# An opening phase in another order: transposes on PE, new load order, x kept in load order

## The chip, the cores and the metric

The kernel runs on one core of one Trainium2 chip. The metric is device time in microseconds (us) of one execution. A core has five engines that run side by side, each strictly in its own order: PE (TensorE, matrix products), DVE (VectorE), ACT (ScalarE), POOL (GpSimd) and SP (SyncE). Here SP issues the plain loads, the stores and the DMA transposes, and POOL issues the loads that change fp32 to bf16 on the way. Work on different engines meets only where one waits for another.

## What is computed

Attention with normalized q and k, and then a feed-forward network with a product in place of an activation. There are 8 batches, 12 heads, 448 tokens and 64 numbers per head; the network has 768 inputs, an inner size of 1,024 and 3,584 tokens.

```python
def rmsnorm(x, g):
    rms = np.sqrt(np.mean(x * x, axis=-1, keepdims=True) + 1e-06)
    return x / rms * g
q_n, k_n = (rmsnorm(q, g_q), rmsnorm(k, g_k))
scores = scale * np.matmul(q_n, k_n.transpose(0, 1, 3, 2))
attn = softmax(scores)                      # written out in the reference
x = np.matmul(attn, v)                      # heads side by side: [3584, 768]
a = x @ w1
b = x @ w2
h = a * b @ w3
return (h @ w_out).astype(np.float32)
```

## The kernel before

**Quads.** Four heads of one batch are a quad; there are 24, three per batch. q and k of a quad are loaded in fp32 as [112, 4 heads, 4, 64] (L86): partition p holds the tokens 4p to 4p+3, so that a token is 4p + j. All score and probability tiles have their columns in the order j, p.

**Preparation of a quad**, in two halves of two heads: squares on POOL (L133; for quad 0 on ACT, L131), their sums on DVE (L136), the inverse root as a logarithm and an exponential on ACT (L141, L143), and the scaling on DVE in three operations (L152, L159, L165), which leaves `qks` in bf16 with tokens on partitions. A DMA transpose from SP (L171) turns it into `qkT`.

**Attention.** A quad has four slots. In each, `qk_exp` makes eight score products (two tiles `sc`, L185) and two exponentials on ACT into P (L194). In the first three slots `pv_set` of the quad before runs (L209): set 0 gives the sums of P, sets 1 and 2 give P times v, which DVE multiplies by the inverse sums into `xT` (L225). This write also changes the columns from the order j, p to the order of the tokens, 4p + j.

**The weights.** w3 and w_out are multiplied first, in 16 units of eight products (`w34_unit`, L240), cast by DVE to `w34s` (L247). For that w3 has to be transposed; eight DMA transposes do it (L353).

**The feed-forward work** is a list of fillers: once the third quad of a batch is through, 16 units of x with w1 or w2 (L254, L271) and the units of the last product (L293) come onto the list, and each slot takes two. DVE copies the result to `o_sb` (L300) and SP stores 128 rows (L303).

**Order.** It is written by hand, and each engine runs its part of it in this order. Before the loop stand quads 0 and 1 and the w3 transposes. Inside the loop quad i's slots hold the preparation of quad i + 2, the loads of q and k of quad i + 3 and of v of quad i + 2. The w34 units run two per slot in quads 1 and 2, fillers from quad 4 on:

```python
        W34_FROM = 1
        FFN_FROM = 4
```

Loads of w1 and w2 (L103) stand on POOL between the squares, four per slot. q, k and v tiles have three and four buffers, the squares two, and the PSUM tiles of w34 units and fillers share two (`mm`). Every eighth load of a queue uses the same semaphore, and an issue waits for the load eight places ahead of it.

## Time and profile before

| | |
|---|---|
| median of 2 runs | 455.52 us (454.74 to 456.31) |
| profiled execution | 451.86 us, its span 450.1 us |
| PE busy | 375.2 us, 83% of the span |
| DVE busy | 288.9 us, 64% |
| ACT busy | 232.5 us, 52% |
| POOL busy | 132.3 us, 29% |
| granted TensorE clock, mean | 0.977 |

The span goes from the first to the last instruction. A busy share is an average over stages that have different limits, so the stages are read apart. In a row of instructions the first number is the start in us from the span's start, then the duration, the engine, the line of the kernel, the operation with what it writes and reads, and how many instructions were merged; in brackets stands how long the engine was idle just before, and what ended that. Issues on SP and POOL show how long the issuing engine was held, not the transfer. Row durations of merged matmuls overlap a little, since matmuls are pipelined.

### The profile page before, as it was taken

What the parts mean: (1) busy time and instruction counts of PE and PEld (TensorE: products, weight loads), DVE (VectorE), ACT (ScalarE), POOL (GpSimd) and SP (SyncE); (2) the same over time, 40 slices, a digit from 0 to 9 for tenths busy, and PEclk for the clock granted to TensorE, in tenths of its full rate; (3) what the DMA queues carried; (4) which work ended last, traced back from release to release, by engine and by line L of the source; (5) the groups of instructions that cost most, each with busy time, mean ns of one, the idle gap of its engine ahead of it and who ended that gap; (6) DMA issues with size and microseconds to landing.
All of it is one profiled execution on the core that took longest, in us unless ns stands there. A gap on an engine that the chain in (4) does not pass through costs nothing.

```text
span 450.1 us, 7194 instructions
## 1 busy us (share of the span) xinstructions
PE 375.2 (83%) x2880; PEld 171.1 (38%) x2880; DVE 288.9 (64%) x380; ACT 232.5 (52%) x357; POOL 132.3 (29%) x148
## 2 busy tenths in 40 slices
PE   0002190796999999999999999999999999999996
PEld 0000040343344544444444444444444454445453
DVE  0531500879577888788877888788888787534333
ACT  3002330456766577556755675568566755673110
POOL 5260802522444124412442144214432340000000
PEclk9999996799799999999999999999999999999999
DMA  8999999555936755686458546954695462201003
GB/s 164 229 176 187 197 175 210 104 119 102 181 36 128 192 115 107 125 231 141 84 118 232 118 75 148 233 121 72 145 215 126 88 167 92 42 0 71 36 0 140
DMA packets 94753, 58.98 MB, mean 131 GB/s; under 512 B 55296, under 2 KB 88576, under 8 KB 94720
## 3 DMA queue, kind: packets, MB, share of 16 engines
q1 hardware_dynamic: 79552, 46.21, 44.3%
q0 software_dynamic: 15168, 12.32, 18.8%
q8 instruction: 22, 0.36, 0.3%
q14 instruction: 11, 0.09, 0.1%
HBM read 46.72 MB, written 11.01 MB: 128 GB/s over the span
## 4 chain that ended last, share of the span: by engine, by line
PE 67%; DMA 10%; DVE 9%; ACT 6%; SPq 4%; POOL 2%; issue 1%; DVEq 0%; POOLq 0%
PE po L293 17%; PE pa L254 14%; PE pb L271 14%; PE pv L209 10%; PE sc L185 8%; ACT P L194 5%; DMA k_sb<-in_k_dram 4%; DVE ssq L136 4%; PE wps L240 4%; DMA w2s<-in_moe_w_dram 2%; DVE xT L225 2%; DMA gk_b<-in_g_k_dram 2%; SPq L353 2%; SPq L171 1%; DVE abT L278 1%; POOL sq L133 1%
## 5 line engine op out<-in xcount | busy, mean ns | idle before, releaser
L194 ACT ACTIVATE P<-sc 112x896 bf16<-112x896 f32 x192 | 164.7, 914 | 59.0 <-PE sc L185 59.0
L185 PE MATMUL sc<-qkT 64*112 64x448 bf16 x384 | 63.1, 387 | 55.4 <-DMA qkT<-qks 33.2
L254 PE MATMUL pa<-xT,w1s 128*128 128x448 bf16 x384 | 85.4, 357 | 2.3 <-DVE xT L225 2.1
L271 PE MATMUL pb<-xT,w2s 128*128 128x448 bf16 x384 | 83.1, 352 | 0.0
L278 DVE TENSOR_TENSOR abT<-pb,a_sb 128x448 bf16<-128x448 f32 x64 | 39.9, 623 | 67.2 <-PE pb L271 46.1
L136 DVE TENSOR_REDUCE ssq<-sq 112x16 f32<-112x1024 f32 x48 | 58.0, 1209 | 34.6 <-POOL sq L133 34.6
L293 PE MATMUL po<-w34s,abT 128*128 128x384 bf16 x448 | 77.1, 326 | 0.1
L97 POOL DMA_DIRECT2D v_sb<-in_v_dram x24 | 18.0, 751 | 183.8 <-PE pv L209 149.2
L141 ACT ACTIVATE lnv<-ssq,eps_t 112x32 f32<-112x32 f32 x24 | 7.7, 321 | 107.8 <-DVE ssq L136 107.8
L133 POOL TENSOR_TENSOR sq<-q_sb 112x512 f32<-112x512 f32 x46 | 49.8, 1083 | 29.6 <-DMA q_sb<-in_q_dram 29.4
L225 DVE TENSOR_TENSOR xT<-pv,r 128x448 bf16<-128x448 f32 x48 | 55.2, 1154 | 3.2 <-PE pv L209 3.2
L185 PEld LDWEIGHTS <-qkT 64*112 64x112 bf16 x384 | 20.2, 127 | 94.8 <-issue 61.6
L293 PEld LDWEIGHTS <-abT 128*128 128x128 bf16 x448 | 42.1, 98 | 34.2 <-issue 8.3
L133 POOL TENSOR_TENSOR sq<-k_sb 112x512 f32<-112x512 f32 x46 | 50.7, 1102 | 7.1 <-DMA k_sb<-in_k_dram 6.9
L152 DVE TENSOR_TENSOR qtmp<-q_sb,alpha 112x512 bf16<-112x512 f32 x48 | 51.1, 1064 | 1.9 <-ACT alpha L143 1.9
L271 PEld LDWEIGHTS <-w2s 128*128 128x128 bf16 x384 | 37.6, 98 | 38.2 <-issue 3.8
L254 PEld LDWEIGHTS <-w1s 128*128 128x128 bf16 x384 | 33.6, 98 | 45.4 <-issue 21.0
L262 ACT CAST a_sb<-pa 128x448 bf16<-128x448 f32 x64 | 34.1, 532 | 26.9 <-PE pa L254 26.9
L209 PE MATMUL pv<-P,v_sb 112*32 112x448 bf16 x768 | 44.9, 355 | 0.0
L300 DVE COPY o_sb<-po 128x384 f32<-128x384 f32 x56 | 30.7, 555 | 21.6 <-PE po L293 21.3
L240 PE MATMUL wps<-w_outs,w3T 128*128 128x384 bf16 x128 | 25.6, 360 | 13.2 <-DVE w34s L247 13.2
L165 DVE TENSOR_TENSOR qks<-k_sb,alpha 112x512 bf16<-112x512 f32 x48 | 36.2, 755 | 0.0
(24 smaller groups left out, 149.9 us busy)
## 6 DMA issues: line engine op xcount, KB each, us to landing
q_sb<-in_q_dram SPq DMA_DIRECT2D x24, 448.0 KB, 4.8
k_sb<-in_k_dram SPq DMA_DIRECT2D x24, 448.0 KB, 5.6
out_dram<-o_sb SPq DMA_DIRECT2D x28, 384.0 KB, 2.7
v_sb<-in_v_dram POOLq DMA_DIRECT2D x24, 224.0 KB, 3.9
w3s<-in_moe_w_dram POOLq DMA_DIRECT2D x8, 256.0 KB, 15.4
w_outs<-in_moe_w_out_dram POOLq DMA_DIRECT2D x4, 384.0 KB, 13.9
w1s<-in_moe_w_dram POOLq DMA_DIRECT2D x8, 192.0 KB, 11.3
w2s<-in_moe_w_dram POOLq DMA_DIRECT2D x8, 192.0 KB, 10.8
```

Source lines behind the costliest of these rows:

```text
L133: nc.gpsimd.tensor_tensor(out=sq[:, t], in0=src[:, hs], in1=src[:, hs], op=MULT)
L136: nc.vector.tensor_reduce(out=s["ssq"][:, :, hs, :], in_=sq, axis=AX, op=ADD)
L152: nc.vector.tensor_tensor(out=qtmp.transpose([0, 2, 1, 3]), in0=s["q"][:, hs], in1=alpha[:, 0, hs].unsqueeze(3).broadcast_to([NP, 2, J, D] ...
L185: nc.tensor.matmul(out=sc[:, u, 0:S], lhsT=qkT[u * D : (u + 1) * D, pr, J + jk, :], rhs=qkT[u * D : (u + 1) * D, pr, 0:J, :].rearrange("d ...
L194: nc.scalar.activation(out=P[:, 2 * pr : 2 * pr + 2, jk, :], in_=sc[:, :, 0:S], func=AF.Exp)
L209: nc.tensor.matmul(out=ps[h * HALF : (h + 1) * HALF, :], lhsT=w, rhs=P[:, h, jk, :], start=(jk == 0), stop=(jk == J - 1), tile_position=(0 ...
L225: nc.vector.tensor_tensor(out=xT[b][:, 2 * m + kind - 1, :].rearrange("d (p j) -> d j p", j=J), in0=ps.rearrange("d (j p) -> d j p", j=J), ...
L240: nc.tensor.matmul(out=ps[:, 0:NH], lhsT=w3T[:, gc, fc * 128 : (fc + 1) * 128], rhs=w_outs[:, gc, nh * NH : (nh + 1) * NH], start=(gc == 0 ...
L254: nc.tensor.matmul(out=ps[:, 0:S], lhsT=w1s[:, c, fi * 128 : (fi + 1) * 128], rhs=xT[b][:, c, :], start=(c == 0), stop=(c == CM - 1),)
L271: nc.tensor.matmul(out=ps[:, 0:S], lhsT=w2s[:, c, fi * 128 : (fi + 1) * 128], rhs=xT[b][:, c, :], start=(c == 0), stop=(c == CM - 1),)
L278: nc.vector.tensor_tensor(out=abT[bp][:, fi, odd * S : (odd + 1) * S], in0=ps[:, 0:S], in1=a_tiles.pop((b, fi)), op=MULT,)
L293: nc.tensor.matmul(out=ps[:, 0:NH], lhsT=abT[bp][:, fi, t * 128 : (t + 1) * 128], rhs=w34s[:, fi, nh * NH : (nh + 1) * NH], start=(fi == 0 ...
```

## The change

- The gains `g_q` and `g_k` are loaded first; quad 0's loads come in halves of two heads; q and k of quads 1 and 2 follow before the loop.
- For quads 0 to 3 the DMA transpose is replaced by 8 PE transposes per half into a PSUM tile and one DVE copy (`prep_pe_transpose`); later quads keep the DMA transpose. The identity for that is made on POOL behind the w_outs loads.
- The eight DMA transposes of w3 are replaced by 8 x 8 PE transposes and eight DVE copies (`w3_transpose`), each one slot ahead of the units that use it.
- Quad 1 is prepared in quad 0's slots, quad 2 in quad 1's, quads 3 and 4 in quad 2's; from then on i + 2 as before. v of quad i + 1 is loaded in quad i.
- The w34 units run from quad 1's third slot to quad 3's second, one w3 transpose and two units per slot. Fillers run from quad 3's third slot on.
- Four loads of w3, and w1 and w2 in turn, stand on POOL two per slot.
- `xT` is written in the order j, p, without permuting. The output rows are then put in place by the stores: each tile of 128 columns is cut where j changes, and each of the two pieces writes rows that lie four rows apart.

```diff
+    out_r = out.rearrange("(b p j) n -> b j p n", b=B, j=J)
-        nc.sync.dma_start_transpose(
-            out=s["qkT"][:, pr], in_=qks.rearrange("p t j h d -> p (t j h d)")
-        )
+        if pe:
+            s["qks", pr] = qks
+        else:
+            nc.sync.dma_start_transpose(
+                out=s["qkT"][:, pr], in_=qks.rearrange("p t j h d -> p (t j h d)")
+            )
+
+    def prep_pe_transpose(i, pr):
+        s = st[i]
+        qks = s.pop(("qks", pr))
+        ps = mm_psum.tile([128, 2 * J, NP], BF, tag="mm", name="qkT_ps")
+        for t in range(2):
+            for j in range(J):
+                nc.tensor.transpose(
+                    ps[:, t * J + j, :], qks[:, t, j], ident[0:NP, 0:NP]
+                )
+        nc.vector.tensor_copy(out=s["qkT"][:, pr], in_=ps)
...
-            out=xT[b][:, 2 * m + kind - 1, :].rearrange("d (p j) -> d j p", j=J),
-            in0=ps.rearrange("d (j p) -> d j p", j=J),
-            in1=s["r"].rearrange("d (j p) -> d j p", j=J),
-            op=MULT,
+            out=xT[b][:, 2 * m + kind - 1, :], in0=ps, in1=s["r"], op=MULT
...
+    def w3_transpose(fc):
+        ps = mm_psum.tile([128, CF, 128], BF, tag="mm", name="w3T_ps")
+        for gc in range(CF):
+            nc.tensor.transpose(
+                ps[:, gc, :], w3s[:, fc, gc * 128 : (gc + 1) * 128], ident
+            )
+        nc.vector.tensor_copy(out=w3T[:, :, fc * 128 : (fc + 1) * 128], in_=ps)
...
-            r0 = bp * TOK2 + t * 128
-            nc.sync.dma_start(out=out[r0 : r0 + 128, :], in_=o_sb)
+            c0 = t * 128
+            while c0 < (t + 1) * 128:
+                c1 = min((c0 // NP + 1) * NP, (t + 1) * 128)
+                bb, j = divmod(c0 // NP, J)
+                p0 = c0 % NP
+                nc.sync.dma_start(
+                    out=out_r[2 * bp + bb, j, p0 : p0 + c1 - c0, :],
+                    in_=o_sb[c0 - t * 128 : c1 - t * 128, :],
+                )
+                c0 = c1
...
+        wq = [lambda c=c: load_w3(c) for c in range(4, CF)]
+        W34_FROM = (1, 2)
...
+            preps = []
+            if i < 3:
+                preps.append(i + 1)
+            if 2 <= i and i + 2 < NQ:
+                preps.append(i + 2)
...
+                if (i, sl) >= W34_FROM and fc_next[0] < CF:
+                    fc = fc_next[0]
+                    if fc == 0:
+                        w3_transpose(0)
+                    if fc + 1 < CF:
+                        w3_transpose(fc + 1)
+                    w34_unit(fc, 0)
+                    w34_unit(fc, 1)
+                    fc_next[0] += 1
+                else:
+                    fill(2)
```

Two places show the order that results. First POOL, from the loads ahead of the loop to the squares of quad 1 (`sq`; `v_sb`, `w3s` are the load targets). The brackets name what an issue waits for: DMASW with a number is the semaphore of an earlier load from POOL, DMAHW of one from SP. Before:

```order
L111 DMA w3s<-in_moe_w_dram 128x1024 x3
L111 DMA w3s<-in_moe_w_dram 128x1024 [waits DMASW0_49]
L111 DMA w3s<-in_moe_w_dram 128x1024 [waits DMASW1_49]
L111 DMA w3s<-in_moe_w_dram 128x1024 [waits DMASW2_49]
L111 DMA w3s<-in_moe_w_dram 128x1024 [waits DMASW3_49]
L111 DMA w3s<-in_moe_w_dram 128x1024 [waits DMASW4_49]
L133 ISA
L133 TENSOR_TENSOR sq<-q_sb 112x512 [waits DMAHW4_49,DVE_49]
L133 TENSOR_TENSOR sq<-k_sb 112x512 [waits DMAHW5_49]
```

After:

```order
L117 DMA w3s<-in_moe_w_dram 128x1024 x3
L117 DMA w3s<-in_moe_w_dram 128x1024 [waits DMASW0_49]
L103 DMA v_sb<-in_v_dram 112x4x256 [waits DMASW1_49]
L139 TENSOR_TENSOR sq<-q_sb 112x512 [waits DMAHW6_49,DVE_49]
L139 TENSOR_TENSOR sq<-k_sb 112x512 [waits DMAHW7_49]
L117 DMA w3s<-in_moe_w_dram 128x1024 [waits DMASW2_49]
L117 DMA w3s<-in_moe_w_dram 128x1024 [waits DMASW3_49]
L139 TENSOR_TENSOR sq<-q_sb 112x512 [waits DVE_49]
L139 TENSOR_TENSOR sq<-k_sb 112x512
L117 DMA w3s<-in_moe_w_dram 128x1024 [waits DMASW4_49]
L117 DMA w3s<-in_moe_w_dram 128x1024 [waits DMASW5_49]
```

Quad 1's squares stood behind all eight w3s loads and together; now they stand in two pairs between the w3s loads, the second pair behind the sixth.

Second DVE, where the weight products begin. Before, in the slots of quad 1 (`w34s` is the cast of a product, `ssq` the sums of squares, `qtmp` and `qks` the scaling):

```order
L247 CAST w34s<-wps 128x384 x2
L136 TENSOR_REDUCE ssq<-sq 112x2x8
L225 TENSOR_TENSOR xT<-pv,r 128x4x112
L247 CAST w34s<-wps 128x384 x2
L136 TENSOR_REDUCE ssq<-sq 112x2x8
L225 TENSOR_TENSOR xT<-pv,r 128x4x112
L247 CAST w34s<-wps 128x384 x2
L152 TENSOR_TENSOR qtmp<-q_sb,alpha 112x2x4x64
L159 TENSOR_TENSOR qks<-qtmp,g_b 112x512
L165 TENSOR_TENSOR qks<-k_sb,alpha 112x2x4x64
```

After, in the last three slots of quad 1 (`qkT_ps` and `w3T_ps` are the PSUM tiles of the PE transposes):

```order
L142 TENSOR_REDUCE ssq<-sq 112x2x8 [waits Pool_49]
L245 TENSOR_TENSOR xT<-pv,r 128x448 [waits PE_49]
L260 COPY w3T<-w3T_ps 128x8x128 [waits PE_49] x2
L272 CAST w34s<-wps 128x384 [waits PE_49] x2
L158 TENSOR_TENSOR qtmp<-q_sb,alpha 112x2x4x64 [waits DMAHW0_49,Activation_49]
L165 TENSOR_TENSOR qks<-qtmp,g_b 112x512 [waits DVE_49]
L171 TENSOR_TENSOR qks<-k_sb,alpha 112x2x4x64 [waits DMAHW1_49]
L193 COPY qkT<-qkT_ps 128x896 [waits PE_49]
L260 COPY w3T<-w3T_ps 128x8x128 [waits PE_49]
L272 CAST w34s<-wps 128x384 [waits PE_49] x2
```

The casts came first and with the reduces of the quad after next between them; now the copies of w3T and the casts stand behind the last reduce of the next quad, and each half's scaling is followed by a copy that waits for PE.

More of the change, by code (lines that the diff above doesn't have):

```diff
@@ L6 @@
 from concourse._compat import with_exitstack
+from concourse.masks import make_identity
 FP = mybir.dt.float32
@@ L321 @@
     with tc.manual_schedule():
-        load_qk(0)
+        nc.sync.dma_start(out=gq_b, in_=g_q.unsqueeze(0).broadcast_to([NP, D]))
+        nc.sync.dma_start(out=gk_b, in_=g_k.unsqueeze(0).broadcast_to([NP, D]))
+        load_qk(0, split=2)
+        load_qk(1)
+        load_qk(2)
         load_v(0)
@@ L326 @@
             load_wout(c)
-        for c in range(2):
+        make_identity(nc, ident)
+        for c in range(4):
             load_w3(c)
-        nc.sync.dma_start(out=gq_b, in_=g_q.unsqueeze(0).broadcast_to([NP, D]))
-        nc.sync.dma_start(out=gk_b, in_=g_k.unsqueeze(0).broadcast_to([NP, D]))
-        load_qk(1)
         nc.vector.memset(eps_t, 64e-6)
```

83 lines of the change are left out of this document (37 added, 46 removed).

## The prediction

> **What bounds the kernel now.** First the busy time by stages, cut where something changes in kind: the first score product, the long stop before 80 us, the first feed-forward product, the last product. The columns are stage and length, then busy us (and count) of PE, weight loads, DVE, ACT and POOL, the granted clock, the DMA share and GB/s.
>
> ```profile
> 0.00:33.17 33.17, 0.00 (x1) 0.00 (x2) 9.28 (x15) 4.68 (x9) 15.90 (x27) 1.00 1.05 191
> 33.17:80.00 46.83, 17.23 (x108) 6.97 (x109) 11.26 (x17) 11.60 (x16) 15.29 (x21) 0.91 1.20 194
> 80.00:117.10 37.10, 32.14 (x249) 14.55 (x248) 31.06 (x43) 21.98 (x32) 13.24 (x15) 0.87 0.58 113
> 117.10:446.10 329.00, 325.78 (x2528) 149.55 (x2524) 236.76 (x305) 194.21 (x300) 87.81 (x87) 1.00 0.52 119
> 446.10:450.10 4.00, 0.01 (x1) 0.00 (x0) 0.56 (x1) 0.00 (x0) 0.00 (x0) 1.00 0.25 98
> ```
>
> From 117.10 on PE is busy for 325.78 of 329.00 us: that stretch can be shortened only by less PE work, and the change takes none away. Up to 117.10 PE is idle for 67.7 us (117.10 - 17.23 - 32.14). The case is decided there. PE's waits of the opening, and the instructions at their ends:
>
> ```profile
> PE sc L185 <- DMA qkT<-qks: 33.2, 1, 33.2
> PE sc L185 <- ACT P L194: 21.4, 15, 15.7
> PE wps L240 <- DVE w34s L247: 13.2, 1, 13.2
> ```
>
> ```profile
> 16.76 8.29 SPq L171 DMA_TRANSPOSE qkT<-qks  x2
> 33.17 0.99 PE L185 MATMUL sc<-qkT 64*112 64x448 bf16 x4 [33.17 <-DMA qkT<-qks]
> 45.48 1.03 POOL L133 TENSOR_TENSOR sq<-k_sb 112x512 f32<-112x512 f32 x1 [3.26 <-DMA k_sb<-in_k_dram]
> 57.95 13.04 SPq L353 DMA_TRANSPOSE w3T<-w3s  x3
> 81.02 4.72 PE L240 MATMUL wps<-w_outs,w3T 128*128 128x384 bf16 x16 [13.18 <-DVE w34s L247]
> 117.10 2.31 PE L254 MATMUL pa<-xT,w1s 128*128 128x448 bf16 x6
> ```
>
> The first scores wait for a DMA transpose issued at 16.76, which lands among the loads 16.4 us later. The 15.7 us named after ACT are the stop at 37 to 53 us: ACT stands in order behind quad 2's norm, whose squares wait for k_sb until 45.48. The 13.2 us named after DVE are the same again for quad 3: its loads stand on SP behind the eight w3 transposes, of which the last three hold SP from 57.95 to 70.99.
>
> **The change, step by step.** I follow the path to the first feed-forward product, called T: 117.10 before. Behind it stands the unchanged PE stream.
>
> *Quad 0.* These rows give the chain from load to scaled operands:
>
> ```profile
> 6.95 0.61 ACT L131 ACTIVATE sq<-k_sb 112x512 f32<-112x512 f32 x1
> 11.63 0.22 DVE L334 TENSOR_TENSOR gq_b<-gq_b,gk_b 112x64 f32<-112x64 f32 x1 [10.69 <-DMA gk_b<-in_g_k_dram]
> 11.99 2.34 DVE L136 TENSOR_REDUCE ssq<-sq 112x16 f32<-112x1024 f32 x2
> 14.37 0.32 ACT L141 ACTIVATE lnv<-ssq,eps_t 112x32 f32<-112x32 f32 x1 [6.80 <-DVE ssq L136]
> 14.98 0.69 DVE L152 TENSOR_TENSOR qtmp<-q_sb,alpha 112x512 bf16<-112x512 f32 x1 [0.65 <-ACT alpha L143]
> 15.71 0.43 DVE L159 TENSOR_TENSOR qks<-qtmp,g_b 112x512 bf16<-112x512 bf16 x1
> 16.05 0.69 DVE L165 TENSOR_TENSOR qks<-k_sb,alpha 112x512 bf16<-112x512 f32 x1
> ```
>
> The squares end at 7.56, and DVE stands until 11.63 for gk_b. With the gains loaded first that goes; two issues ahead of q cost about 0.5. Reduce to 9.1, norm 0.65, one scaling 1.76 (14.98 to 16.74): 11.6. Then transposes and copy, the second scaling, transposes: the first scores at 16 instead of 33.17. This alone ends nothing sooner: quads 1 and 2 are next. On SP the transposes of w3 and of quads 0 to 3 leave the queue, so quad 3's loads go out once quad 0 has been scaled, about 15, and no longer behind 70.99.
>
> *Quads 1 and 2 through POOL.* POOL has eight loads in flight; a ninth waits for the first. These issues show the landing of v, of the first and fourth w_outs and of the sixth w3s:
>
> ```profile
> 10.72 0.53 POOL L111 DMA_DIRECT2D w3s<-in_moe_w_dram  x1 [4.06 <-DMA v_sb<-in_v_dram]
> 13.31 0.53 POOL L111 DMA_DIRECT2D w3s<-in_moe_w_dram  x1 [2.06 <-DMA w_outs<-in_moe_w_out_dram]
> 21.38 0.53 POOL L111 DMA_DIRECT2D w3s<-in_moe_w_dram  x1 [2.03 <-DMA w_outs<-in_moe_w_out_dram]
> 29.91 0.56 POOL L103 DMA_DIRECT2D w1s<-in_moe_w_dram  x1 [0.81 <-DMA w3s<-in_moe_w_dram]
> ```
>
> So a w3s takes (29.91 - 21.38)/6 = 1.42 us. In the new order quad 1's second squares stand behind the twelfth load, which waits for the third w_outs (about 18.7); I put its scores at 31. Quad 2's second squares stand behind the load that waits for the seventh w3s: 21.38, seven w3s 9.9, the v load between them 2.5 and the share of the extra q and k about 1.5, so 35.3. Issue 0.5, squares 2 x 1.08, reduce 1.21: DVE is free at 39.1. PE's first weight slot stands behind that reduce, since DVE takes its copies of w3T after it.
>
> *Eight weight slots* (two weight products each) then lead to T. Their prices:
>
> ```profile
> 86.25 2.71 PE wps L240 x16
> 88.89 0.59 PE L185 MATMUL sc<-qkT 64*112 64x448 bf16 x4
> 89.40 0.94 PE L209 MATMUL pv<-P,ones 112*32 112x448 bf16 x16
> L247 DVE CAST w34s<-wps 128x384 bf16<-128x384 f32 x16 | 8.7, 556 | 10.6 <-PE wps L240 10.6
> L136 DVE TENSOR_REDUCE ssq<-sq 112x16 f32<-112x1024 f32 x12 | 14.5, 1213 | 34.6 <-POOL sq L133 34.6
> L133 POOL TENSOR_TENSOR sq<-k_sb 112x512 f32<-112x512 f32 x11 | 11.9, 1082 | 5.3 <-DMA k_sb<-in_k_dram 5.3
> L293 PEld LDWEIGHTS <-abT 128*128 128x128 bf16 x448 | 42.1, 98 | 34.2 <-issue 8.3
> L225 DVE TENSOR_TENSOR xT<-pv,r 128x448 bf16<-128x448 f32 x42 | 48.3, 1154 | 3.2 <-PE pv L209 3.2
> L278 DVE TENSOR_TENSOR abT<-pb,a_sb 128x448 bf16<-128x448 f32 x64 | 39.9, 623 | 67.2 <-PE pb L271 46.1 <-PE sc L185 14.5 <-ACT a_sb L262 6.6
> ```
>
> Eight PE transposes are not in this trace. Their weight loads alone are 8 x 98 ns = 0.8 us; as eight matmuls of 326 ns one behind the other they would be 2.6. I take 1.0, near the weight loads. The copy out of PSUM has two bounds: at the rate between the cast and the abT row (67 ns for 64 more elements, about 1.05 ns each) 896 elements cost 1.09 us and 1,024 cost 1.22; at the step from L152 to L159 (half the bytes, 0.43 for 0.69), 0.62 and 0.69. L159 is the row with bf16 in and out, as these copies are, so I take 0.6 and 0.67.
>
> The Trainium skill ("VectorE: DVE Perf Modes", "Why PSUM operands drop a tier") says that a PSUM operand limits a copy to two elements a cycle at best and to one in fp32. By that the lower prices hold; at the upper ones T would be 5 us later. No row here shows a bf16 copy out of PSUM.
>
> PE and DVE hand work back and forth in both orders, so a slot is a chain, not the longer sum. A slot with a preparation: scores 0.59, w3 transposes 1.0, two products 2.71, last cast 0.56, scaling 1.76, q/k transposes 1.0, hand-overs 0.1 = 7.7; with PV 0.94 it is 8.6. Four slots are of this kind: the first, begun with a cold PE as at 81.02, at 10.0, two at 7.7, one (quad 2's third) at 8.6. Quad 2's first slot runs over DVE's copy 0.6, the reduces of quads 3 and 4 (2 x 1.21), the w3T copy 0.67 and the second product 1.36: 5.3 with hand-overs. Its second adds scores, PV and xT (0.59 + 0.94 + 0.62) in place of that first copy: 6.7. Quad 3's first goes over quad 4's scaling 1.76, copy 0.6, reduce 1.21, copy 0.67 and a product 1.36: 5.7; its second is PE alone, 0.59 + 0.94 + 2.71 = 4.2. Sum: 10.0 + 7.7 + 5.3 + 6.7 + 8.6 + 7.7 + 5.7 + 4.2 = 55.9. With one more scores and PV, 1.5: T = 39.1 + 55.9 + 1.5 = 96.5. For a clock that falls in some waits I add 3 (bounds 0 and the 2.0 between the two wps rows for each of eight slots, 16): **T = 99.5**.
>
> *Behind T.* Two slots of scores and one PV set, done before 117.10 in the old program, now come later: +2.1; the six pa at 2.31 us, in a stretch where PE had just been idle, become about 1.2: -1.1. Fillers begin two slots sooner, the first batch has 22, so one slot late in quad 6 stands empty; the flush at the end has the same 24. Keeping x in load order makes the xT write plain: 48 x (1154 - 623 ns) = 25 us of DVE, but hidden by PE; PE waited 3.2 us in all behind 117.10, so I take 1.0 off (bounds 0 and 3.2). The output rows go out as 56 stores for 28. SP has room, and each piece still moves whole rows; only the end counts, where one more issue stands ahead of the last piece:
>
> ```profile
> 446.73 0.33 SPq L303 DMA_DIRECT2D out_dram<-o_sb  x1
> ```
>
> That is +0.4. Nothing else moved has a price: w1 and w2 go out in quads 0 to 2 and have landed by about 66, well ahead of T; v goes out one quad ahead, some 15 us against a landing of 4 to 15; quad 4's DMA transposes have two quads of slack. POOL's identity, about 2 us, only pushes w3s back.
>
> Sum: 450.1 - (117.1 - 99.5) + 2.1 - 1.1 - 1.0 + 0.4 = 432.9 us of span, 17.2 less. The profiled execution took 451.86, 3.66 below the median 455.52 of the two runs; on that scale the forecast is **438 us**.
>
> **Rivals.** *The clock stays at half (slower).* With PE waiting in every slot, its matmuls may stay at the slow rate throughout. Slow and fast rows:
>
> ```profile
> 113.30 0.62 PE L185 MATMUL sc<-qkT 64*112 64x448 bf16 x2 [0.19 <-ACT P L194]
> 115.48 1.69 PE L209 MATMUL pv<-P,ones 112*32 112x448 bf16 x16
> 106.60 0.40 PE L185 MATMUL sc<-qkT 64*112 64x448 bf16 x2 [0.41 <-ACT P L194]
> ```
>
> At the slow ones a slot is 1.24 + 1.69 + 2.0 + 4.72 = 9.7 on PE alone, and in four of the eight 4.3 more (cast, scaling, transposes at 2.0): T = 39.1 + 8 x 9.7 + 4 x 4.3 = 134, by the same sum the end 17 us above before, 473 on the median's scale. It makes the kernel slower once the slots average above 9.5 us. Against it: at 106.60 PE is at full rate with gaps on both sides. Chance 0.08. The Trainium skill ("TensorE: Matmul & The Clock Gate", Part 4) gives about 275 ns for a transpose in one kernel and says that transposes do not count as activity that raises the clock, which speaks for this rival; by 275 ns a set of eight is 2.2 us and T some 8 us later. This trace holds no PE transpose.
>
> *Loads of q and k starve.* Beside the weight stream a k load took up to 19.2 us:
>
> ```profile
> DMA to landing us min/median/max: 4.4/5.6/19.2
> ```
>
> If quads 1 and 2 each take that long behind quad 0 (done at 7), quad 2 lands at 45 and DVE is free at 49: T 109, the end at 448. Chance 0.17, since the early q and k now have only v and w_outs beside them.
>
> *PE alone sets the slots.* If DVE's part is covered, a slot is PE's 0.59 + 0.94 + 1.0 + 2.71 = 5.2: T = 39.1 + 8 x 5.2 + 1.5 = 82, the end at 421. Chance 0.12; the order of both engines speaks against it.
>
> **How the numbers follow.** Forecast 0.63, with T from 92 to 106: 430 to 445. Above 423 and below 452 lie nearly all of it, the starved loads, and half of the PE-bound case; left out are the half clock, half of the PE-bound case and a rest, about 0.16. A change of 2% (446.4 and 464.6) is about what a measurement here can tell. Faster: 0.60 of the forecast, 0.12, and a fifth of the starved loads, about 0.76; same 0.17; slower 0.07, the half clock less its mild end.
>
> **What would show it.** First scores near 16 us, quad 1's near 31, quad 2's near 57; DVE's reduce of quad 2 ending near 39; weight products at 1.36 us for eight; T near 99; xT near 0.62 us; PE almost without idle behind T. It is wrong if quad 2's squares come after 45 us, if slots average above 8.5 us, or if the stretch behind T is not about 330 us long.

## The result, and the profile after

The changed kernel took 430.93 us in the median of two runs (429.42 to 432.44), against 455.52 us before. The ratio is 0.946, with a 95% interval of 0.930 to 0.962: faster by about 5%. The profiled execution took 432.44 us with a span of 430.7 us. The times of e2 and e7 below each leave out one execution at a lower clock; in e7 it is the profiled one, so that its trace is not used.

The stages after, cut at the first score product, the end of DVE's last reduce of quad 2, the first feed-forward product (T) and the last copy of a product. The columns are those of the table in the prediction.

```profile
0.00:21.72 21.72, 2.15 (x16) 1.27 (x16) 7.16 (x13) 4.35 (x7) 8.37 (x17) 1.00 0.96 195
21.72:45.93 24.21, 12.88 (x93) 4.75 (x93) 14.72 (x14) 11.69 (x16) 16.72 (x24) 1.00 1.15 242
45.93:99.79 53.86, 42.82 (x357) 22.43 (x353) 35.86 (x56) 18.96 (x30) 19.33 (x22) 0.90 0.49 95
99.79:425.69 325.90, 324.12 (x2552) 148.49 (x2548) 226.95 (x312) 199.21 (x305) 95.80 (x88) 1.00 0.59 121
425.69:430.70 5.01, 0.00 (x0) 0.00 (x0) 0.56 (x1) 0.00 (x0) 0.00 (x0) 0.86 0.33 97
```

T came at 99.79, 17.3 us sooner than before. Up to T, PE was idle for 67.7 us before; now it is 41.9 (99.79 less 2.15, 12.88 and 42.82). It is busier up to T (57.9 us for 49.4) because the transposes of w3 and of the first quads are now its own, although two slots of scores and one set of PV now stand behind T. Behind T the stretch went from 329.00 to 325.90, and the end behind the last copy from 4.00 to 5.01. The sum is 17.3 + 3.1 - 1.0 = 19.4, the whole difference of the spans (450.1 and 430.7).

PE's waits up to 105 us in the changed kernel (total, times, longest) answer to the three shown of before:

```profile
PE qkT_ps L190 <- DVE qks L165: 34.6, 8, 17.5
PE qkT_ps L190 <- DVE qks L171: 3.1, 5, 2.2
PE wps L265 <- DVE w3T L260: 2.5, 3, 1.8
```

The three stops of 33.2, 15.7 and 13.2 us are gone. In their place PE waits for scaled operands: 17.5 us at the very start, and then many times for 1.7 to 4.6 us. Where they lie is seen in the instructions of the opening, here PE (transposes of q and k, scores, weight products), ACT (the squares of quad 0), POOL (the squares of quads 1 and 2) and DVE (the second scaling of quad 1, an xT write, the last reduce of quad 2). A slot's four score products are one row (x4; two to a `sc` tile, so four to a slot and not eight):

```profile
13.76 0.63 ACT L137 ACTIVATE sq<-k_sb 112x512 f32<-112x512 f32 x1 [1.89 <-DMA k_sb<-in_k_dram]
21.72 0.99 PE L205 MATMUL sc<-qkT 64*112 64x448 bf16 x4
23.78 1.04 POOL L139 TENSOR_TENSOR sq<-k_sb 112x512 f32<-112x512 f32 x1 [4.20 <-DMA k_sb<-in_k_dram]
32.79 2.70 DVE L158 TENSOR_TENSOR qtmp<-q_sb,alpha 112x512 bf16<-112x512 f32 x1
32.89 1.05 POOL L139 TENSOR_TENSOR sq<-q_sb 112x512 f32<-112x512 f32 x1
33.89 1.04 POOL L139 TENSOR_TENSOR sq<-k_sb 112x512 f32<-112x512 f32 x1
35.87 2.85 DVE L171 TENSOR_TENSOR qks<-k_sb,alpha 112x512 bf16<-112x512 f32 x1
37.11 1.04 POOL L139 TENSOR_TENSOR sq<-k_sb 112x512 f32<-112x512 f32 x1
39.26 0.99 PE L205 MATMUL sc<-qkT 64*112 64x448 bf16 x4
44.18 0.62 DVE L245 TENSOR_TENSOR xT<-pv,r 128x448 bf16<-128x448 f32 x1 [3.06 <-PE pv L229]
44.72 1.21 DVE L142 TENSOR_REDUCE ssq<-sq 112x16 f32<-112x1024 f32 x1
47.34 2.77 PE L265 MATMUL wps<-w_outs,w3T 128*128 128x384 bf16 x16 [0.34 <-DVE w3T L260]
61.51 0.59 PE L205 MATMUL sc<-qkT 64*112 64x448 bf16 x4
99.79 1.31 PE L279 MATMUL pa<-xT,w1s 128*128 128x448 bf16 x6
```

The last half load of quad 0 lets ACT square only at 13.76 (6.95 before), the first k of quad 1 is squared at 23.78, and two scaling operations of quad 1 take 2.70 and 2.85 us where the same operations took 0.69 in quad 0 before. Both of these lie beside squares on POOL. The first scores of quads 0, 1 and 2 come at 21.72, 39.26 and 61.51; in the old order the first of these stood at 33.17. DVE's last reduce of quad 2 (44.72) doesn't wait for its squares, which ended at 38.15 (37.11 + 1.04). It stands in order behind the xT write at 44.18, and that waited 3.06 for PE's PV, which comes after quad 1's scores.

### The profile page after: what moved, and what is told of

Its sections match the earlier page's. It is cut to its first block, busy times and chain, and to the rows that moved or that the text cites. A ratio compares the mean times of both kernels' runs of the same rounds, so it can differ in the third digit from the quotient of the medians.

```text
span 430.7 us, 7455 instructions
## 1 busy us (share of the span) xinstructions
PE 382.0 (89%) x3008; PEld 176.9 (41%) x3008; DVE 285.2 (66%) x396; ACT 234.2 (54%) x357; POOL 140.2 (33%) x150
## 4 chain that ended last, share of the span: by engine, by line
PE 81%; DVE 8%; DMA 4%; ACT 2%; issue 1%; POOL 1%; SPq 1%; DVEq 0%
PE pa L279 18%; PE pb L296 17%; PE po L318 16%; PE pv L229 13%; PE sc L205 10%; PE wps L265 5%; DMA k_sb<-in_k_dram 4%; DVE qtmp L158 2%; DVE ssq L142 2%; ACT P L214 2%; DVE qks L171 2%; DVE qks L165 1%; POOL sq L139 1%; SPq L92 1%; PE w3T_ps L257 1%
## 5 line engine op out<-in xcount | busy, mean ns | idle before, releaser
L139 POOL TENSOR_TENSOR sq<-q_sb 112x512 f32<-112x512 f32 x46 | 53.9, 1171 | 192.5 <-DMA q_sb<-in_q_dram 172.9
L279 PE MATMUL pa<-xT,w1s 128*128 128x448 bf16 x384 | 83.7, 354 | 0.0
L303 DVE TENSOR_TENSOR abT<-pb,a_sb 128x448 bf16<-128x448 f32 x64 | 39.7, 621 | 63.5 <-PE pb L296 45.0
L142 DVE TENSOR_REDUCE ssq<-sq 112x16 f32<-112x1024 f32 x48 | 57.9, 1211 | 11.8 <-ACT sq L137 7.5
L205 PE MATMUL sc<-qkT 64*112 64x448 bf16 x384 | 60.6, 388 | 2.8 <-ACT P L214 2.8
L139 POOL TENSOR_TENSOR sq<-k_sb 112x512 f32<-112x512 f32 x46 | 54.5, 1186 | 7.6 <-DMA k_sb<-in_k_dram 7.3
L171 DVE TENSOR_TENSOR qks<-k_sb,alpha 112x512 bf16<-112x512 f32 x48 | 49.3, 1027 | 0.0
L287 ACT CAST a_sb<-pa 128x448 bf16<-128x448 f32 x64 | 33.6, 525 | 22.3 <-PE pa L279 22.3
L325 DVE COPY o_sb<-po 128x384 f32<-128x384 f32 x56 | 30.1, 552 | 22.4 <-PE po L318 22.4
L158 DVE TENSOR_TENSOR qtmp<-q_sb,alpha 112x512 bf16<-112x512 f32 x48 | 42.3, 881 | 1.3 <-ACT alpha L149 1.3
L245 DVE TENSOR_TENSOR xT<-pv,r 128x448 bf16<-128x448 f32 x48 | 29.9, 622 | 18.3 <-PE pv L229 17.6
L190 PE MATMUL qkT_ps<-ident,qks 112*128 112x112 bf16 x64 | 7.6, 259 | 37.9 <-DVE qks L165 34.6
L205 PEld LDWEIGHTS <-qkT 64*112 64x112 bf16 x384 | 18.5, 129 | 37.8 <-issue 36.8
L165 DVE TENSOR_TENSOR qks<-qtmp,g_b 112x512 bf16<-112x512 bf16 x48 | 31.9, 665 | 1.6
```

The source lines that it names most:

```text
L139: nc.gpsimd.tensor_tensor(out=sq[:, t], in0=src[:, hs], in1=src[:, hs], op=MULT)
L142: nc.vector.tensor_reduce(out=s["ssq"][:, :, hs, :], in_=sq, axis=AX, op=ADD)
L158: nc.vector.tensor_tensor(out=qtmp.transpose([0, 2, 1, 3]), in0=s["q"][:, hs], in1=alpha[:, 0, hs].unsqueeze(3).broadcast_to([NP, 2, J, D] ...
L171: nc.vector.tensor_tensor(out=qks[:, 1].transpose([0, 2, 1, 3]), in0=s["k"][:, hs], in1=alpha[:, 1, hs].unsqueeze(3).broadcast_to([NP, 2, ...
L205: nc.tensor.matmul(out=sc[:, u, 0:S], lhsT=qkT[u * D : (u + 1) * D, pr, J + jk, :], rhs=qkT[u * D : (u + 1) * D, pr, 0:J, :].rearrange("d ...
L279: nc.tensor.matmul(out=ps[:, 0:S], lhsT=w1s[:, c, fi * 128 : (fi + 1) * 128], rhs=xT[b][:, c, :], start=(c == 0), stop=(c == CM - 1),)
```

## The experiments

The measured places of the runs that are compared below, in us from the start: the first scores of quads 0 and 1, the first weight product, T, then the median time and the ratio to the runs of before beside it. The places are read from one trace of each kernel. In e1, e3, e4 and e5, whose work up to there is that of the changed kernel, the first scores stand at 22.3 to 22.4 and not at 21.7; so a difference in T of less than 1 us is not read as an effect. The runs of before beside them had medians from 454.8 to 459.8 us; times of different sets are therefore better compared by the ratio.

| kernel | q0 | q1 | wps | T | time | ratio, 95% interval |
|---|---|---|---|---|---|---|
| before | 33.2 | 55.1 | 58.1 | 117.1 | 455.52 | |
| changed | 21.7 | 39.3 | 47.3 | 99.8 | 430.93 | 0.946 (0.930 to 0.962) |
| e1 x in token order | 22.3 | 39.9 | 49.0 | 98.9 | 433.93 | 0.946 (0.939 to 0.953) |
| e2 hold the weights | 22.9 | 36.5 | 47.2 | 99.3 | 430.76 | 0.937 (0.927 to 0.946) |
| e3 quad 2's squares on ACT | 22.4 | 35.7 | 44.2 | 99.2 | 432.48 | 0.942 (0.936 to 0.949) |
| e4 scaling ahead of the products | 22.3 | 39.7 | 47.8 | 94.0 | 426.85 | 0.929 (0.923 to 0.935) |
| e5 w3 by DMA | 22.4 | 40.1 | 59.6 | 113.5 | 445.60 | 0.972 (0.964 to 0.979) |
| e6 q and k by DMA | 35.0 | 58.7 | 66.8 | 110.4 | 443.20 | 0.967 (0.959 to 0.975) |
| e8 hold, more on ACT | 17.4 | 35.7 | 43.7 | 92.7 | 423.78 | 0.923 (0.917 to 0.930) |
| e9 the same, squares later | 17.3 | 30.5 | 39.0 | 86.7 | 418.63 | 0.921 (0.916 to 0.926) |
| e10 e9 without the hold | 22.2 | 35.4 | 43.8 | 87.7 | 420.43 | 0.925 (0.921 to 0.929) |
| e11 e9, quad 4 later | 17.4 | 30.6 | 39.0 | 85.5 | 418.19 | 0.919 (0.913 to 0.926) |

The old kernel began its weight products at 58.1, but after four of the 16 units it stood until 81.0, the stop that the prediction shows.

### e1: x in token order again

```diff
-            out=xT[b][:, 2 * m + kind - 1, :], in0=ps, in1=s["r"], op=MULT
+            out=xT[b][:, 2 * m + kind - 1, :].rearrange("d (p j) -> d j p", j=J),
+            in0=ps.rearrange("d (j p) -> d j p", j=J),
+            in1=s["r"].rearrange("d (j p) -> d j p", j=J),
...
+            r0 = bp * TOK2 + t * 128
+            nc.sync.dma_start(out=out[r0 : r0 + 128, :], in_=o_sb)
```

> The changed kernel with x written in the order of the tokens again and 28 plain stores. The theory that x's order was worth what DVE's idle PE waits show (1.0 in the forecast, 3 by the stretch behind the first feed-forward product, 325.9 us against 329.0 forecast): that stretch becomes 328 to 330, the xT row 1.15 us, the first feed-forward product stays at 100 to 102, the end of the stores 0.5 to 1 us nearer to the last product; total 2 to 4 us above the changed kernel. Rival (x's order is where the gain behind the opening comes from and more): stretch above 333, total 6 us or more above. Rival (x's order only costs, by 56 stores): total no higher or lower.

Measured: 433.93 us in the median of four (433.46 to 437.77), ratio 0.946 (0.939 to 0.953); span 431.7. Its last two stages, from T (98.85) to the last copy and from there to the end, and the group of the xT writes (busy us, mean ns, idle before):

```profile
98.85:427.87 329.02, 325.34 (x2552) 148.36 (x2548) 243.43 (x313) 199.13 (x305) 93.61 (x88) 1.00 0.56 120
427.87:431.70 3.83, 0.00 (x0) 0.00 (x0) 0.56 (x1) 0.00 (x0) 0.00 (x0) 0.93 0.26 103
L245 DVE TENSOR_TENSOR xT<-pv,r 128x448 bf16<-128x448 f32 x48 | 55.4, 1157 | 17.5 <-PE pv L229 17.3
```

With the write of 1,157 ns the stretch behind T is 329.02 long, with the plain one (mean 622 ns) 325.90. So the order of x is worth 3.1 us there, and 1.2 (5.01 - 3.83) are given back at the end by the stores in pieces. Net it is about 2 us of the 19.4; nearly all of the gain lies ahead of T. The times alone don't show the 2 us: the ratio is that of the changed kernel, and in this trace T came 0.9 sooner, so that its span is only 1.0 longer.

### e2: the weights held back

POOL's first load waits until quad 1's k has landed, by a multiplication that reads it.

```diff
+        hold = const.tile([NP, 2, J, D], FP, name="hold")
+        nc.gpsimd.tensor_tensor(
+            out=hold, in0=st[1]["k"][:, 0:2], in1=st[1]["k"][:, 0:2], op=MULT
+        )
         load_v(0)
```

> The changed kernel with POOL's first load held until quad 1's k has landed, by one extra multiply that reads it. Theory (quad 0 and quad 1 are late because their loads share the DMA with v and w_outs: k of quad 0 landed by 13.8 us, k of quad 1 at 23.7): quad 0's k lands by 8, quad 1's by 12, quad 0's first scores come near 15 for 21.7, quad 1's near 30 for 39.3; the weights come some 6 us later than they did but ahead of need, the first feed-forward product near 93 for 99.8, total 5 to 8 us below the changed kernel. Rival (the loads of q and k are slow by themselves, behind the gains or by their halves): quad 1's k still lands at 18 or later, the first product is at 100 or later, total the same or up to 6 us above.

Measured: 430.76 us (429.92 to 432.03), T 99.26, where 93 was expected. ACT's last square of quad 0, the hold and the end of the identity:

```profile
9.64 0.63 ACT L137 ACTIVATE sq<-k_sb 112x512 f32<-112x512 f32 x1 [0.17 <-DMA k_sb<-in_k_dram]
13.35 1.46 POOL L362 TENSOR_TENSOR hold<-k_sb 112x512 f32<-112x512 f32 x1 [12.90 <-DMA k_sb<-in_k_dram]
18.81 0.29 POOL masks.py:199 TENSOR_SCALAR_AFFINE_SELECT ident<-ident 128x128 bf16<-128x128 bf16 x1
```

Without v and weights beside it the last half of quad 0 is squared 4.1 us sooner (9.64 for 13.76), and quad 1's k is there by 13.35, where its square had to wait until 23.78. That the loads of v and the weights starved these loads is shown. The transposes of quad 0 didn't profit, since the identity stood behind the hold (a side effect of this edit). Quad 1 came 2.7 sooner (36.54), and yet T is within 0.5 of the changed kernel's: the first weight product stood at 47.22 for 47.34, because quad 2's squares, behind the weight loads on POOL, came at 39.58 to 44.8. A gain at one place of the chain was lost at the next.

### e3: quad 2's squares on ACT

```diff
-                        prep_sq(n, sl)
+                        if n != 2:
+                            prep_sq(n, sl)
...
+                if (i, sl) == (0, 3):
+                    prep_sq(2, 0, on_act=True)
+                    prep_sq(2, 1, on_act=True)
```

> The changed kernel with quad 2's squares on ACT at the end of quad 0 in place of POOL. Theory (two scaling operations of quad 1, 2.70 and 2.85 us for 0.69, are slow because POOL's squares run beside them): both become 0.7, quad 1's first scores come near 35 for 39.3, the first feed-forward product near 95.5 for 99.8, total 4 us below the changed kernel. Rival (those operations wait for something else, a DMA write or PE's read): they stay above 2 us, total within 1 us.

Measured: 432.48 us (431.62 to 435.49), T 99.19, where 95.5 was expected. The two scaling operations of quad 1 now take 0.68 and 0.69 us, with no squares beside them. From the first scores of quad 0 to those of quad 1 it is 13.35 us (22.39 to 35.74) and not 17.54: 4.2 less, just what the two operations had lost (2.0 + 2.2). But the same happened one quad on. DVE's scaling of quad 2 and POOL's squares beside it:

```profile
33.45 0.68 DVE L158 TENSOR_TENSOR qtmp<-q_sb,alpha 112x512 bf16<-112x512 f32 x1
34.51 0.69 DVE L171 TENSOR_TENSOR qks<-k_sb,alpha 112x512 bf16<-112x512 f32 x1
48.19 4.72 DVE L165 TENSOR_TENSOR qks<-qtmp,g_b 112x512 bf16<-112x512 bf16 x1
48.59 1.05 POOL L139 TENSOR_TENSOR sq<-q_sb 112x512 f32<-112x512 f32 x1
51.58 1.03 POOL L139 TENSOR_TENSOR sq<-k_sb 112x512 f32<-112x512 f32 x1
```

Four squares run back to back on POOL from 48.59 to 52.61 and an operation that takes 0.42 us alone takes 4.72. PE waited 6.00 for it at 52.96. The first weight product stood 3.1 us sooner than in the changed kernel, and at T that was lost again (99.19 for 99.79).

### e4: the scaling ahead of the weight products

In the changed kernel DVE scales quads 2 and 3 at the end of a slot, after the casts of that slot's weight products, and PE waits for it each time. Here the scaling stands ahead of the products.

```diff
+                    early = [n for n in preps if sl >= 2 and n < 4]
+                    for n in early:
+                        prep_scale(n, sl - 2, pe=True)
                     w34_unit(fc, 0)
                     w34_unit(fc, 1)
```

> The changed kernel with the scaling of quads 2 and 3 ahead of the two weight products of its slot in place of behind them. Theory (in four of the eight weight slots PE and DVE hand the work back and forth, and PE stands 1.7 to 2.5 us for the scaling): these slots go from 7.2 to 8.2 us down to about 6, the slow clock after two of the waits goes too, the first feed-forward product near 92 for 99.8, total 6 to 8 us below the changed kernel. Rival (the slots are set by DVE's sum or by the clock, not by the order of the two): slots stay above 7, total within 2 us.

Measured: 426.85 us (425.64 to 427.59), T 93.97, where 92 was expected. PE's waits of 1.7 to 2.5 us for scaled operands of quads 2 and 3 are gone but for one. That one is in these rows of DVE and PE; the scaling lies again beside POOL's squares (47.95 to 51.98):

```profile
48.26 4.28 DVE L158 TENSOR_TENSOR qtmp<-q_sb,alpha 112x512 bf16<-112x512 f32 x1
54.12 0.55 PE L190 MATMUL qkT_ps<-ident,qks 112*128 112x112 bf16 x8 [3.54 <-DVE w34s L272]
```

The chain of DVE and PE sets the slots, as the prediction had it; taking four of its links off the chain gave 5.8 us at T.

### e5 and e6: one kind of transpose by DMA

e5 takes the w3 transposes back to DMA, e6 those of q and k of quads 0 to 3, both at the places of the new order.

```diff
-        for gc in range(CF):
-            nc.tensor.transpose(
...
-        nc.vector.tensor_copy(out=w3T[:, :, fc * 128 : (fc + 1) * 128], in_=ps)
+        nc.sync.dma_start_transpose(
+            out=w3T[:, :, fc * 128 : (fc + 1) * 128], in_=w3s[:, fc, :]
+        )
```

> Edit: w3 is transposed by DMA again, from SP, at the very places of the changed order; everything else is the changed kernel. Question: does the gain hang on the PE transposes of w3 or on the order? In before a transpose of a w3 chunk landed 8.7 us after its issue (median of 8). Theory PE (the PE transposes carry it): the first weight product then waits 8.7 us and not about 2, and every later slot is at least as long as one transpose, 8.7 us against 6.7; T = 45.9 + 8.7 + 7 x 8.7 + 4 = 119, time near 450. Theory order (the place carries it): only the first product waits longer, +6.7, and eight slots lose 0.62 of PE work each, so T is 99.8 + 6.7 - 4 = 102.5 and the time 433 to 436.

```diff
-                        pe = n < 4
+                        pe = False
```

> Edit: quads 0 to 3 get their q/k transposes by DMA from SP, as before had them, at the changed order's places; w3 stays on PE. A DMA transpose of such a pair landed 4.4 us after its issue in before (median of 12); the PE way took 1.16 + about 1.3 with its copy in the cold stage. Theory cheap: the first scores of quads 0 and 1 come about 2 later each, and the four preparing slots lose PE's waits of 1.7 to 2.5 us for the scaled values, because a DMA transpose has a slot to land in: T 95 to 98, time 426 to 430, so PE transposes of q and k are not what gained. Theory queue: the transposes stand on SP behind loads that wait for their buffers, and the DMA traffic of the opening (240 GB/s) stretches them to 10 us and more: T 108 to 118, time 440 to 450.

Measured: e5 445.60 us (444.18 to 448.24), T 113.53; e6 443.20 us (442.47 to 445.37), T 110.36. The rows of SP and PE show it, first for e5, then for e6 (a second number on SP is how long the issue held it):

```profile
39.68 17.57 SPq L255 DMA_TRANSPOSE w3T<-w3s  x3
59.63 4.43 PE L262 MATMUL wps<-w_outs,w3T 128*128 128x384 bf16 x16 [12.82 <-DMA w3T<-w3s]
```

```profile
18.78 11.24 SPq L180 DMA_TRANSPOSE qkT<-qks  x2
34.97 0.99 PE L205 MATMUL sc<-qkT 64*112 64x448 bf16 x4 [34.97 <-DMA qkT<-qks]
```

In e5 three transposes hold SP for 17.57 us. The first product waits 12.82, more than the 8.7 that I had taken from the median of before, and the result lies between my two theories, nearer to the one that PE transposes carry the gain. In e6 the numbers are those of the theory of the queue: quad 0's transposes, issued from 18.78, let the first scores go only at 34.97, later than in the old kernel (33.17). Only its second half is seen, though: SP waited for DVE's scaling with these issues, not for loads ahead of them, and it is the transposes themselves that took so long. So both kinds on PE are needed for the whole gain. With the new order and only the q and k transposes on PE, T gains 3.6 over before (117.1 to 113.5); with the new order and only those of w3, 6.7; with both 17.3. What the order gives with neither was not tried.

### e7 and e8: ACT takes the squares

e7 is e4 with the squares of quad 2 (as in e3) and of quad 3 on ACT. e8 adds the hold of e2 behind the identity, and quad 1's squares on ACT.

```diff
+        make_identity(nc, ident)
+        hold = const.tile([NP, 2, J, D], FP, name="hold")
...
-                        prep_sq(n, sl)
+                        if n != 2:
+                            prep_sq(n, sl, on_act=n in (1, 3))
...
+                if (i, sl) == (0, 3):
+                    prep_sq(2, 0, on_act=True)
+                    prep_sq(2, 1, on_act=True)
```

> Edits: the scaling of quads 2 and 3 ahead of the weight products (as in e4), the squares of quad 2 on ACT at the end of quad 0 (as in e3), and the squares of quad 3 on ACT too, so that POOL squares nothing while DVE scales quad 2. Theory collision (DVE's scaling is slow only beside POOL's squares): the ops of 2.6 and 2.8 us of quad 1 and the one of 4.3 us of quad 2 become 0.68; with e4's T of 93.97 less 3.6 (quad 1, as e3's first full scores came 3.5 earlier) less 3.6 (quad 2) T is 86 to 88 and the time 418 to 421. Rival: the long scaling ops come from the DMA traffic or from the clock of the stage, not from POOL; then they stay, T is 92 to 95 and the time 425 to 428. Rival: ACT's extra squares (8 of 0.63) delay the exponentials and scores by as much; T 90 to 92.

> e7, and POOL makes the identity first and then holds its loads of v and weights until quad 1's k has landed (as in e2, whose identity stood behind the hold); the squares of quad 1 are on ACT too. Theory starvation (q and k of the first quads starve beside the weight stream): quad 0's first scores at 16 to 17 (21.7 in the changed kernel, 22.9 in e2 for its identity), quad 1's at 25 to 28, first weight slot near 36; T 80 to 84, time 412 to 416. Rival: the weights held back for 13 us are then late themselves: w3 and w_out (3.5 MB at about 240 GB/s, 15 us) land only near 30 to 35 and the w1, w2 chunks after them, so that the slots wait for weights: T 86 to 90, time 418 to 422, no better than e7.

Measured: e7 429.47 us (429.35 to 430.88), ratio 0.937 (0.929 to 0.944); its time misses the two that were expected (418 to 421, 425 to 428), and it is slower than e4 by 2.6 us, though the intervals of the two ratios overlap. e8 423.78 us (422.28 to 425.06), T 92.70. In e8 the first scores came at 17.38, 4.3 sooner than in the changed kernel, and not one scaling operation up to the last weight slot was above 0.7 us; both as the theories have it. The expected 80 to 84 for T wasn't reached because the reduces now waited for ACT, and other work stood behind them on DVE:

```profile
31.11 2.35 DVE L142 TENSOR_REDUCE ssq<-sq 112x16 f32<-112x1024 f32 x2 [2.72 <-ACT sq L137]
34.56 1.16 PE L190 MATMUL qkT_ps<-ident,qks 112*128 112x112 bf16 x8 [5.92 <-DVE qks L165]
55.75 2.35 DVE L142 TENSOR_REDUCE ssq<-sq 112x16 f32<-112x1024 f32 x2 [3.54 <-ACT sq L137]
58.74 1.76 PE L265 MATMUL wps<-w_outs,w3T 128*128 128x384 bf16 x5 [3.96 <-DVE w3T L260]
```

Quad 2's reduces stand ahead of quad 1's second scaling, and quad 3's ahead of a copy of w3T; PE waits 5.92 and 3.96 for what is behind them. e7 has the same squares of quads 2 and 3 at the same places, which I take for the cause of its miss; that is not shown.

### e9, e10 and e11: the reduces out of the way

e9 is e8 with ACT's squares of quads 2 and 3 behind the scaling of the last slot of quads 0 and 1. e10 is e9 without the hold.

```diff
-                            prep_sq(n, sl, on_act=n in (1, 3))
+                        if n not in (2, 3):
+                            prep_sq(n, sl, on_act=n == 1)
...
                             prep_pe_transpose(n, sl - 2)
+                if sl == 3 and i < 2:
+                    prep_sq(i + 2, 0, on_act=True)
+                    prep_sq(i + 2, 1, on_act=True)
```

> e8 with ACT's squares of quads 2 and 3 put behind the scaling of the slot that ends quad 0 and quad 1 (in e8 the reduces of quad 2 stood on DVE ahead of quad 1's second scaling, 31.11 to 33.37, while PE waited 5.92; those of quad 3 stood ahead of a w3T copy while PE waited 3.96 and 2.92). Theory order (a reduce that waits on DVE is what PE waits for): quad 1's second pair of scores at 30 to 31 (35.65 in e8), no wait over 2 for a w3T copy, T = 92.7 - 5 - 6 = 81 to 83, time 411 to 414. Rival weights: the w3 chunks held back land after 33 to 40 and the first weight slot, now near 37, waits for them; T 86 to 89, time 416 to 420.

> The same as e9 without the hold, the identity made where the changed kernel makes it. Against e9 it prices the starved q and k loads alone, now that nothing behind takes the gain back. Theory starvation: quad 0's first scores at 21 to 22 and quad 1's near 31 to 33, 4 to 5 later than in e9, and T as much later: 86 to 88, time 417 to 420. Rival (the head start is lost again, as in e2): T and the time are those of e9 within 2.

Measured: e9 418.63 us (417.70 to 419.41), T 86.73; e10 420.43 us (419.50 to 420.77), T 87.71. The order theory holds as far as quad 2: quad 1's scores stand at 30.53 (35.65 in e8) and the first weight product at 38.98 (43.73). But then quad 4 is late, and T and the time of e9 are those of the rival, though not at the place that it named (the first weight slot waited for no load). In e9 the last load issue ahead of quad 4's squares on POOL, DVE's reduce of quad 4 and the product behind it, and in e10 the last two:

```profile
50.76 0.73 POOL L103 DMA_DIRECT2D v_sb<-in_v_dram  x1 [0.70 <-DMA w1s<-in_moe_w_dram]
53.59 1.22 DVE L142 TENSOR_REDUCE ssq<-sq 112x16 f32<-112x1024 f32 x1 [3.89 <-POOL sq L139]
55.46 2.72 PE L265 MATMUL wps<-w_outs,w3T 128*128 128x384 bf16 x8 [5.43 <-DVE w3T L260]
```

```profile
55.58 1.22 DVE L142 TENSOR_REDUCE ssq<-sq 112x16 f32<-112x1024 f32 x1 [1.03 <-POOL sq L139]
57.45 2.72 PE L265 MATMUL wps<-w_outs,w3T 128*128 128x384 bf16 x8 [2.58 <-DVE w3T L260]
```

e9 is 4.85 us ahead of e10 at the scores of quads 0 and 1 and at the first weight product, 2.0 at the product in these rows (55.46 and 57.45) and 1.0 at T. So the expected T of e10 (86 to 88) was met, but the rival was right about the difference: starved q and k loads cost about 5 us at the front and only 1.0 at T, and 1.8 in the time. What took the head start back is seen on POOL. In e9 quad 4's squares follow at 51.51 at once on the issue at 50.76, which, like the issues before it, waited for an earlier load; the hold had put all these loads later. In e10 POOL was through with such issues by 47.0, and its squares waited until 53.51 for DVE's reduce of quad 3, which frees their buffer (its row stands in the last section). e11 moves quad 4's squares and reduces behind the weight products of their slots:

```diff
+                if i == 2 and sl < 2:
+                    prep_sq(4, sl)
+                    if sl == 1:
+                        prep_alpha(4)
```

> e9 with the squares and reduces of quad 4 behind the weight products of their slots. In e9 the reduce of quad 4 stood on DVE ahead of a w3T copy and waited 3.89 for POOL's squares of a quad whose k landed late (53.59), and PE waited 5.43 for that copy. Theory order: PE's wait goes down to the 0.6 to 0.9 of the other slots, T = 86.7 - 4.8 = 82, time 413 to 415. Rival: the late reduce only moves the wait to quad 4's scaling two slots on, T stays within 1.5 of 86.7 and the time at 417 to 419.

Measured: 418.19 us (417.81 to 420.52), ratio 0.919 (0.913 to 0.926), T 85.46. The rival again: the wait moved one slot on (not two), and is only 0.9 shorter.

```profile
57.19 1.22 DVE L142 TENSOR_REDUCE ssq<-sq 112x16 f32<-112x1024 f32 x1 [4.74 <-POOL sq L139]
59.59 2.72 PE L265 MATMUL wps<-w_outs,w3T 128*128 128x384 bf16 x8 [4.50 <-DVE w3T L260]
```

POOL's squares stand in its queue behind the last w1 and w2 loads and a v load, each of which waits for one eight places ahead; a run with fewer loads ahead of quad 4's squares was not tried. e9 and e11 are both faster than the changed kernel by about 12 us (418.6 and 418.2 against 430.9, ratios 0.921 and 0.919 against 0.946), and can't be told apart by their ranges.

## Why the prediction was right, and where it was not

**The size.** Forecast 438 in a range of 423 to 452, measured 430.93. Of the 7 us, 2.3 belong to the profiled executions: 434.7 was forecast on that scale (451.86 - 17.2), and it was 432.44. The rest is how one execution stands to its median. I added 3.66, because the profiled execution of before lay that much below; the one after lay 1.5 above. That step carried a run's spread into the forecast.

**T, 99.5 forecast and 99.79 measured: two errors that cancel.** DVE was free of quad 2's reduce at 45.93 and not at 39.1, 6.8 later; the slots took 53.86 us and not 60.4 (55.9 + 1.5 + 3). That T was met to 0.3 us is luck. Of the signs of being wrong none came: the last square of quad 2 began at 37.11, the eight slots took 6.6 us on average, and the stretch behind T was 325.9 long.

**The step "DVE is free at 39.1" failed.** It followed quad 2's squares alone, and these came as forecast: the last ended at 38.15, for 38.0 (35.3 + 0.5 + 2.16). But DVE works in order, and ahead of its last reduce stands an xT write that needs PE's PV of the slot, and with it quad 1's scores. From those scores to the end of the reduce it took 6.7 us (39.26 to 45.93). Had quad 1 come at 31, that path would have ended at 37.7, ahead of the squares; it became the later one because quad 1 was 8.3 late. In e3, with quad 1's scores 3.5 sooner, PE's first w3 transposes start 3.1 sooner (42.78).

**The step "two issues ahead of q cost about 0.5" failed.** It put the first scores at 16; they came at 21.72. The loads of quad 0 are not alone: quads 1 and 2, v and the weights run beside them, and the last half is squared at 13.76. e2 shows that 4.1 of this come from the loads of v and the weights. The step "quad 1's second squares stand behind the twelfth load", 31 for its scores, failed for the same cause (k squared at 23.78), and for one I didn't look for, scaling beside squares on POOL. 2.70 and 2.85 for 0.69 each are 4.2 us more, and e3, with those squares gone from POOL, has them back.

**The rival of starved loads** had quad 2 land at 45, DVE free at 49 and T at 109. The starving was there in quads 0 and 1 (e2), and the w3 loads stood beside these too. Quad 2 was not late by its loads: its squares were done at 38.15. So the 45.93 lies nearer to the rival's 49 than to my 39.1 by another path, through quad 1.

**The slots were priced right in kind, the first and the fifth too high.** By the starts of the scores that end them (53.54, 61.51, 66.53, 73.03, 80.26, 88.47, 94.31, 98.40, the first from 45.93):

| slot | 1 | 2 | 3 | 4 | 5 | 6 | 7 | 8 | last scores, PV |
|---|---|---|---|---|---|---|---|---|---|
| forecast | 10.0 | 7.7 | 5.3 | 6.7 | 8.6 | 7.7 | 5.7 | 4.2 | 1.5 |
| measured | 7.6 | 8.0 | 5.0 | 6.5 | 7.2 | 8.2 | 5.8 | 4.1 | 1.4 |

Two sizes were off. A set of eight w3 transposes takes 0.62 us and not 1.0 in a busy stretch (1.04 at the slow clock), and the eight of a half of q and k take 2 x 0.37. And the clock: the first slot, priced cold at 10.0, ran warm, and only the second and the sixth are slow for most of their length. The rows are transposes and weight products of the changed kernel in the second, the fifth (fast) and the sixth slot:

```profile
54.24 1.04 PE L257 MATMUL w3T_ps<-ident,w3s 128*128 128x128 bf16 x8
55.07 3.82 PE L265 MATMUL wps<-w_outs,w3T 128*128 128x384 bf16 x16
74.42 0.62 PE L257 MATMUL w3T_ps<-ident,w3s 128*128 128x128 bf16 x8
74.88 2.76 PE L265 MATMUL wps<-w_outs,w3T 128*128 128x384 bf16 x16
81.33 4.34 PE L265 MATMUL wps<-w_outs,w3T 128*128 128x384 bf16 x16
```

The excesses over the fast rows are 0.42 + 1.06 and 1.58, 3.1 us in all, and the scores and PV that begin the seventh slot add about 1.2 (0.99 and 1.69 us at 88.47 and 89.39, for 0.59 and 0.94). I had taken 3, and 2.3 more in the cold price of the first slot.

**PE alone sets the slots** (T 82) didn't happen. It had 43.1 us for the slots (8 x 5.2 + 1.5). From the first w3 transpose to T the changed kernel took 53.86, e4 47.57, e9 49.16 and e10, with the scaling off the chain, no collisions and no loads held back, 45.29. T of e9 is lower still, since its slots begin 4.85 sooner than those of e10. Of e9's 49.16 PE is busy for 40.02:

```profile
37.57:86.73 49.16, 40.02 (x356) 21.40 (x353) 34.35 (x56) 19.48 (x32) 20.53 (x28) 0.93 0.80 153
```

**The half clock** is refuted for this order: the granted clock was 0.90 in the slot stage, and no slot is above 8.2 us. The copies out of PSUM came at the lower bounds (0.62 and 0.68 to 0.69 us), so the Trainium skill's rule on PSUM operands ("VectorE: DVE Perf Modes", "Why PSUM operands drop a tier") agrees with this trace. Its 275 ns for a transpose ("TensorE: Matmul & The Clock Gate", Part 4) would make 2.2 us of a set of eight; the measurement, 0.62, decides.

**Behind T**, 329.0 were forecast (+2.1 - 1.1 - 1.0) and 325.90 measured. By e1 the plain xT write is worth 3.1 and not the 1.0 I took: the upper bound, 3.2, was right. The two other terms (+2.1 and -1.1) came out at 0 together and not at +1.0 (e1's 329.02 against before's 329.00). The end cost 1.0 more than before, and I had 0.4.

## What to carry to other kernels

Where two engines hand work back and forth, a gain at the head of the chain shows at its end only if no later link is late for another reason: here 4.85 us at the first scores were worth 1.0 at T (e9 against e10), and moving a scaling of 1.8 us off the chain in four slots was worth more (5.8, e4). Look at what stands in order behind a waiting reduce or a slow operation before you move its producer. And be wary of a price from a quiet row: a pair of q/k transposes by DMA that landed in 4.4 us in the median of before let the scores wait 16.2 among the loads of e6 (18.78 to 34.97), as the first of before had done (16.4), and a scaling of 0.42 us took 4.72 beside a busy POOL.

## What the runs showed of the hardware

**DVE's scaling is held up while POOL squares.** An operation of 0.42 to 0.69 us took 2.70, 2.85, 4.28 and 4.72 beside two or four squares back to back, and ended 0.3 to 0.6 us behind the last of them; POOL's squares stayed at 1.03 to 1.05. With these squares taken from POOL (e8) every scaling up to the last weight slot took at most 0.69. Not every DVE operation is hit. In e10, DVE's reduces and a copy out of PSUM beside POOL's squares:

```profile
52.22 2.33 DVE L142 TENSOR_REDUCE ssq<-sq 112x16 f32<-112x1024 f32 x2
53.51 1.04 POOL L139 TENSOR_TENSOR sq<-q_sb 112x512 f32<-112x512 f32 x1 [6.48 <-DVE ssq L142]
56.66 1.05 POOL L139 TENSOR_TENSOR sq<-q_sb 112x512 f32<-112x512 f32 x1
56.72 0.68 DVE L260 COPY w3T<-w3T_ps 128x1024 bf16<-128x1024 bf16 x1
```

They keep their 1.2 and 0.68 us. The Trainium skill ("SBUF — State Buffer", "Who interferes with whom") says that a DVE instruction with two inputs in SBUF contends with a GpSimd instruction that reads SBUF, and that a reduce, or one with a single SBUF input outside the two-port modes, does not. All these rows agree. It also says that the order of issue decides which of the two blocks; here DVE's operation at 32.79 began, by the starts in the rows, 0.1 us ahead of the square at 32.89 and still ended 0.6 after the second one.

**A DMA transpose among loads is slow and holds its queue.** Three w3 transposes held SP for 17.57 us (e5) and two of q and k for 11.24 (e6), while the DMA moved 203 and 240 GB/s in all. Loads of q and k of 448 KB starve likewise: in the first 50 us of the changed kernel the median k took 18.7 us to land, over the whole kernel 6.2.
